# Hash attention and gated layers on one core: the first head prepared in halves, its hash weights on POOL, the second head scaled and rounded on ACT

## The chip, the core and the metric

The kernel runs on one core of a Trainium2 chip. Its engines run side by side: TensorE (PE, with its weight loads as PEld), VectorE (DVE), ScalarE (ACT), GpSimd (POOL) and SyncE (SP, which issues most transfers). Each takes its instructions in order and waits for the others through semaphores. The metric is the device time of one execution, in microseconds (us).

## What is computed

Attention over 4 batches of 8 heads (768 tokens, head size 64) with a mask from hash buckets, then two matrix products with a gate between them:

```python
q_bits = (np.einsum('bhsd,dk->bhsk', q, proj) > 0)      # 6 bits for each token; k alike
mask = q_bucket[:, :, :, None] == k_bucket[:, :, None, :]
scores = np.where(mask, scale * np.matmul(q, k.transpose(0, 1, 3, 2)), -1000000000.0)
attn = softmax(scores); x = np.matmul(attn, v)          # then (B*S, H*D) = (3072, 512)
h = x @ w_in; g = h * np.clip(h + 3.0, 0.0, 6.0) / 6.0  # 2048 wide
return g @ w_out
```

## The kernel before

PE multiplies in a rounded 32-bit format. Each factor is therefore held as a high part (the rounded value) and a low part (the rest), and a product is a sum of two or three matmuls. For head `i`, the tile `raw{i}` holds the transposed queries (rows 0 to 63) and keys (rows 64 to 127). `split_qk` makes from it four blocks of 128 x 768 in two tiles, `kk` (k1, k2) and `qq` (q1, q2): high parts, copies of them on the other rows, and low parts. `scale_q` multiplies the query rows by -1/8 first.

`hash_qk` multiplies these blocks with the projection: `pjl` (low parts) and `pjh` (high parts) are the stationary side, and the result `z` is made in two halves of 384 columns, three matmuls each (L330, L331, L332). `bits` turns the signs of `z` into rows 64 to 107 of q1 (L341, on DVE), and twelve of these rows are copied into k1 (L346, on ACT, for the first head; a transfer for the others). With these rows in place, one product of q1 with k1 (L376) gives score and mask together; q2 with k2 (L378) adds the low parts and does not need the bits.

The scores of one block of 128 queries, numbered `g`, go through a row of steps: `lowest` (L385, DVE, the minimum), `exponential` (L397, ACT), `transp` (L407, PE, six transposes), `split_p` (L464 on ACT, L468 on DVE, high and low part), `values` (L489, PE) and `output`. The loop over `k` works on several blocks at a time: in step `k` it transposes block `k`, starts the exponential of `k+1` and the scores of `k+3`. A head has six blocks. The hash of head `n` is issued when the scores of the fourth block of head `n-1` are, so head 1's stands on PE right behind the first six transposes. After the heads of one batch the two matrix products (`gemm1`, L634; `gemm2`, L673 to L678) are laid beside the next batch's heads.

The order on PE, DVE, ACT and POOL is the order of the code. The start is written out: 30 transposes of an identity matrix without use of the result (`NWARM`, L144), then `split_qk(0)`, `hash_qk(0)`, `bits(0)`, `scale_q(1)`, `split_v(0)` and three calls of `ahead`, the first of which calls `lead(0)` and with it `split_qk(1)`. For head 0, ACT and DVE make all blocks, and DVE makes the hash weights (`hash_weights`, L258 to L262) between two of its pieces. For head 1, POOL scales (L276, four pieces), rounds (L304) and makes the low parts (L318, four pieces for the keys, four for the queries); SP copies the rounded rows to the other half of the tiles.

## Time and profile before

| What | Value |
|---|---|
| Runs: median, lowest, highest | 1000.93, 998.02, 1001.17 us (3 runs) |
| The profiled execution: time, span | 998.6 us, 996.8 us |
| Busy share: PE, DVE, ACT, POOL | 96%, 74%, 63%, 50% |
| Chain that ended last: PE, DVE, issue, ACT, DMA, POOL | 61%, 17%, 6%, 5%, 4%, 4% |

PE is busy nearly all the time, and the chain of waits lies on it for most of the span. The busy time of PE is modelled and counts matmuls that overlap in its pipeline, so 96% does not mean that no more work would fit in. The shares are means over the whole span; what the change touches lies in the first 20 us, which have to be read by themselves.

### The profile page before, as it was taken

What the parts mean: (1) busy time and instruction counts of PE and PEld (TensorE: products, weight loads), DVE (VectorE), ACT (ScalarE), POOL (GpSimd) and SP (SyncE); (2) the same over time, 40 slices, a digit from 0 to 9 for tenths busy, and PEclk for the clock granted to TensorE, in tenths of its full rate; (3) what the DMA queues carried; (4) which work ended last, traced back from release to release, by engine and by line L of the source; (5) the groups of instructions that cost most, each with busy time, mean ns of one, the idle gap of its engine ahead of it and who ended that gap; (6) DMA issues with size and microseconds to landing.
All of it is one profiled execution on the core that took longest, in us unless ns stands there. A gap on an engine that the chain in (4) does not pass through costs nothing.

```text
span 996.8 us, 19354 instructions
## 1 busy us (share of the span) xinstructions
PE 960.7 (96%) x6330; PEld 876.2 (88%) x6330; DVE 739.9 (74%) x1439; ACT 632.2 (63%) x1419; POOL 495.6 (50%) x520
## 2 busy tenths in 40 slices
PE   8999999999999999799999999999999999999997
PEld 7999889888889998689989898898889989899996
DVE  7999988988579999777878878878877863243322
ACT  6889866555478887566666766666666663333332
POOL 6787735556546776455655654645645542100100
PEclk9999999999999999999999999999999999999999
DMA  4557679000044554488788787777788670101000
GB/s 120 145 151 178 155 213 379 9 2 1 7 131 115 122 122 122 129 231 240 225 260 246 219 252 224 227 234 226 236 236 239 197 215 14 43 1 43 1 22 22
DMA packets 109900, 148.38 MB, mean 149 GB/s; under 512 B 13364, under 2 KB 79284, under 8 KB 109800
## 3 DMA queue, kind: packets, MB, share of 16 engines
q1 hardware_dynamic: 105320, 141.64, 47.0%
q0 software_dynamic: 4480, 5.51, 4.4%
q8 instruction: 50, 0.82, 0.3%
q14 instruction: 50, 0.41, 0.1%
HBM read 75.76 MB, written 51.90 MB: 128 GB/s over the span
## 4 chain that ended last, share of the span: by engine, by line
PE 61%; DVE 17%; issue 6%; ACT 5%; DMA 4%; POOL 4%; SPq 3%; DVEq 0%; ACTq 0%; POOLq 0%
PE h L634 17%; PE acc L489 6%; PE pt L407 5%; PE po L678 5%; PE po L673 5%; PE po L674 5%; PE s L376 4%; PE s L378 4%; DVE p L385 4%; PE acc L501 4%; SPq L78 3%; DVE pl L468 3%; DMA px<-fd 2%; DVE gb L664 2%; POOL pl L466 2%
## 5 line engine op out<-in xcount | busy, mean ns | idle before, releaser
L397 ACT ACTIVATE p<-p,m 128x768 f32<-128x768 f32 x192 | 180.2, 939 | 90.7 <-DVE p L385 83.6
L385 DVE TENSOR_SCALAR_CACHE_REDUCE p<-s 128x768 f32<-128x768 f32 x192 | 182.9, 953 | 42.1 <-PE s L378 26.2
L656 DVE SCALAR_TENSOR_TENSOR g<-g,h 128x256 f32<-128x256 f32 x192 | 80.1, 417 | 104.8 <-ACT g L655 103.3
L655 ACT ACTIVATE g<-h,three 128x256 f32<-128x256 f32 x192 | 90.9, 473 | 94.9 <-PE h L634 80.2
L634 PE MATMUL h<-xh,w 128*128 128x256 f32 x1024 | 146.4, 283 | 2.9 <-ACT xh L624 2.9
L634 PEld LDWEIGHTS h<-xh,w 128*128 128x128 f32 x1024 | 135.7, 189 | 6.2 <-ACT xh L624 3.1
L466 POOL TENSOR_TENSOR pl<-spare,ph 128x384 fp32r<-128x384 f32 x43 | 58.9, 1370 | 120.2 <-ACT ph L464 84.1
L418 DVE STREAM_TRANSPOSE p<-p 128x768 f32<-128x768 f32 x86 | 84.0, 977 | 43.5 <-ACT p L397 43.5
L663 ACT CAST gb<-g 128x256 fp32r<-128x256 f32 x139 | 56.4, 406 | 80.4 <-DVE g L656 52.4
L468 DVE TENSOR_TENSOR pl<-pt,ph 128x384 fp32r<-128x384 f32 x204 | 104.0, 549 | 3.7 <-ACT ph L464 3.2
L376 PE MATMUL s<-kk,qq 76*128 76x384 f32 x384 | 101.5, 345 | 4.2 <-DVE qq L341 2.4
L464 ACT CAST ph<-pt 128x384 fp32r<-128x384 f32 x204 | 89.9, 474 | 17.5 <-PE pt L407 14.4
L378 PE MATMUL s<-kk,qq 128*128 128x384 f32 x384 | 100.1, 342 | 0.0
L673 PE MATMUL po<-w,gb 128*128 128x512 f32 x246 | 96.9, 394 | 0.4 <-ACT gb L663 0.4
L216 POOL TENSOR_TENSOR w<-wr,w 128x128 fp32r<-128x128 f32 x128 | 73.7, 609 | 47.2 <-ACT w L210 47.0
L674 PE MATMUL po<-w,gb 128*128 128x512 f32 x246 | 96.8, 394 | 0.0
L407 PE MATMUL pt<-ident,p 128*128 128x128 f32 x636 | 89.7, 274 | 5.9 <-DVE pl L468 4.4
L664 DVE TENSOR_TENSOR gb<-g,gb 128x256 fp32r<-128x256 f32 x136 | 77.8, 572 | 18.6 <-ACT gb L663 18.2
L407 PEld LDWEIGHTS pt<-ident,p 128*128 128x128 f32 x636 | 74.4, 140 | 15.0 <-PE pt L407 3.7
L634 PE MATMUL h<-xl,w 128*128 128x256 f32 x512 | 83.6, 283 | 2.6 <-POOL xl L625 2.2
L466 POOL TENSOR_TENSOR pl<-px,ph 128x384 fp32r<-128x384 f32 x43 | 56.1, 1304 | 56.7 <-ACT ph L464 42.7
L678 PE MATMUL po<-w,gb 128*128 128x512 f32 x246 | 78.2, 399 | 3.2 <-DVE gb L664 3.1
(156 smaller groups left out, 2167.8 us busy)
## 6 DMA issues: line engine op xcount, KB each, us to landing
fd<-p SPq DMA_DIRECT2D x86, 384.0 KB
spare<-fd SPq DMA_DIRECT2D x172, 96.0 KB
px<-fd SPq DMA_DIRECT2D x172, 96.0 KB
kk<-qq SPq DMA_DIRECT2D x62, 192.0 KB
wr<-in_w_in SPq DMA_DIRECT2D x16, 512.0 KB
wr<-in_w_out SPq DMA_DIRECT2D x16, 512.0 KB
raw<-in_qkT SPq DMA_DIRECT2D x20, 384.0 KB
vr<-in_v SPq DMA_DIRECT2D x32, 192.0 KB
```

What stands on the lines that cost most here:

```text
L376: nc.tensor.matmul(s[:, c, :HW], lhsT=q1[:KM, us], rhs=half(k1[:KM], c), start=True, stop=False)
L378: nc.tensor.matmul(s[:, c, :HW], lhsT=q2[:, us], rhs=half(k2, c), start=False, stop=True)
L385: nc.vector.tensor_scalar(out=pr_[:], in0=s[:, :, :HW], scalar1=CAP, scalar2=None, op0=ALU.min, op1=ALU.min, accum_out=m[:],)
L397: nc.scalar.activation(pr_[:], pr_[:], AF.Exp, bias=m[:], scale=-1.0, accum_out=sms[b][:, t, h : h + 1])
L407: nc.tensor.transpose(pt[:, x], probs[g][0][:, c, x * P : (x + 1) * P], ident[:])
L466: engine.tensor_sub(lo, pt, hi.bitcast(F32))
L468: lows.append(lambda: engine.tensor_sub(lo, pt, hi.bitcast(F32)))
L634: nc.tensor.matmul(hp[:], lhsT=wi[:, wp, wc], rhs=x[cc][xp], start=(k == 0 and cc == 0), stop=(k == 2 and cc == NCC - 1),)
L664: engine.tensor_sub(gl, g[:], gh.bitcast(F32))
L673: nc.tensor.matmul(po[u], lhsT=gh[:, us], rhs=wo[:, 0], start=(fc == 0), stop=False)
L674: nc.tensor.matmul(po[u], lhsT=gh[:, us], rhs=wo[:, 1], start=False, stop=False)
L678: nc.tensor.matmul(po[u], lhsT=gl[:, us], rhs=wo[:, 0], start=False, stop=(fc == NFC - 1))
```

## The change

The constant `NWARM` goes from 30 to 23. Of the steps for head 0: `hash_weights` runs on POOL, ahead of everything else of this head; ACT makes its three blocks in halves, in the order that the first half of the hash takes them; the bits of the first half are issued between the two halves of the hash; and the scores of head 0 take q2 with k2 first, then q1 with k1. Of head 1: ACT scales the queries in one piece and rounds both (L274, L305 of the new file), where POOL did. Lines move by up to four; the order of everything after the first two heads is the same as before.

```diff
-NWARM = 30
+NWARM = 23
...
     def hash_weights():
         for x in range(2):
             c = ZK + (1 - x) * NB
-            nc.vector.tensor_scalar_mul(pjh[:, c : c + NB], pr[:], (1.0, -1.0)[x])
+            nc.gpsimd.tensor_scalar_mul(pjh[:, c : c + NB], pr[:], (1.0, -1.0)[x])
         for r, c in ((slice(0, D), D), (slice(D, P), ZK)):
             pos = pjh[r, ZK + NB : ZM]
-            nc.vector.tensor_sub(pjl[r, c + NB : c + 2 * NB], pr[r], pos.bitcast(F32))
-            nc.vector.tensor_sub(pjl[r, c : c + NB], pos.bitcast(F32), pr[r])
+            nc.gpsimd.tensor_sub(pjl[r, c + NB : c + 2 * NB], pr[r], pos.bitcast(F32))
+            nc.gpsimd.tensor_sub(pjl[r, c : c + NB], pos.bitcast(F32), pr[r])
...
-        n = 4 if i <= 2 else 1
+        n = 4 if i == 2 else 1
...
-            if paced:
+            if paced or i == 1:
                 nc.scalar.mul(raws[i][:D, c], raws[i][:D, c], -SCALE)
...
         if i == 0:
 
+            hash_weights()
+            both = (slice(0, HW), slice(HW, S))
             nc.scalar.mul(q1[:D], raw[:D], -SCALE)
             nc.vector.tensor_copy(q1[D:], raw[D:])
-            for c in (slice(0, HW), slice(HW, S)):
+            for c in both:
                 nc.vector.tensor_sub(k2[:D, c], raw[D:, c], q1[D:, c].bitcast(F32))
-                if c.start == 0:
-                    hash_weights()
                 nc.vector.scalar_tensor_tensor(
                     out=q2[D:, c], in0=raw[:D, c], scalar=-SCALE, in1=q1[:D, c].bitcast(F32),
                     op0=ALU.mult, op1=ALU.subtract,
                 )
-            nc.scalar.copy(k2[D:], raw[D:])
-            nc.scalar.copy(q2[:D], q1[:D].bitcast(F32))
-            nc.scalar.copy(k1[:D], raw[D:])
+                nc.scalar.copy(k2[D:, c], raw[D:, c])
+                nc.scalar.copy(q2[:D, c], q1[:D, c].bitcast(F32))
+            for c in both:
+                nc.scalar.copy(k1[:D, c], raw[D:, c])
...
         for j in range(2):
+            if i == 0 and j:
+                bits(0, (0,))
...
-    def bits(i: int):
+    def bits(i: int, js=(slice(0, 2),)):
...
-        for c in range(2):
-            nc.tensor.matmul(s[:, c, :HW], lhsT=q1[:KM, us], rhs=half(k1[:KM], c), start=True, stop=False)
-        for c in range(2):
-            nc.tensor.matmul(s[:, c, :HW], lhsT=q2[:, us], rhs=half(k2, c), start=False, stop=True)
+        terms = [(q1[:KM], k1[:KM]), (q2, k2)]
+        if i == 0:
+            terms.reverse()
+        for n, (x, y) in enumerate(terms):
+            for c in range(2):
+                nc.tensor.matmul(s[:, c, :HW], lhsT=x[:, us], rhs=half(y, c), start=n == 0, stop=n == 1)
...
-            split_qk(n, nc.scalar.copy if ffn_on else nc.gpsimd.tensor_copy)
+            split_qk(n, nc.scalar.copy if ffn_on or n == 1 else nc.gpsimd.tensor_copy)
...
-        bits(0)
+        bits(0, (1,))
```

The order on ACT at the start, before (`qq_143` and `kk_142` are head 0's tiles, `p_197` is the first block of scores):

```order
L290 ACTIVATE qq_143<-raw_89 64x768 [waits DMAHW0_49]
L300 CAST kk_142<-raw_89 64x768
L301 CAST qq_143<-qq_143 64x768 [waits Activation_49]
L302 CAST kk_142<-raw_89 64x768
L346 CAST kk_142<-qq_143 12x384 [waits DVE_49] x2
L397 ACTIVATE p_197,sms_199<-p_197,m_196 128x768 [waits DVE_49]
```

And after (`raw_127` and `qq_171` are head 1's, the rest as above):

```order
L292 ACTIVATE qq_136<-raw_89 64x768 [waits DMAHW0_49]
L300 CAST kk_135<-raw_89 64x384
L301 CAST qq_136<-qq_136 64x384 [waits Activation_49]
L303 CAST kk_135<-raw_89 64x384 x2
L348 CAST kk_135<-qq_136 12x384 [waits DVE_49] x2
L274 ACTIVATE raw_127<-raw_127 64x768 [waits DMAHW3_49]
L305 CAST qq_171<-raw_127 128x768 [waits Activation_49]
L401 ACTIVATE p_190,sms_192<-p_190,m_189 128x768 [waits DVE_49]
```

The three whole copies have become six halves, and two instructions of head 1 now stand between the copy of the bits and the first exponential.

The order on POOL at the start, before (`raw_134`, `kk_177`, `qq_178` are head 1's, `vr_136` head 0's values):

```order
L276 TENSOR_SCALAR raw_134<-raw_134 64x192 [waits DMAHW3_49]
L356 CAST vv_174<-vr_136 128x6x64 [waits DMAHW4_49]
L357 TENSOR_TENSOR vv_174<-vr_136,vv_174 128x6x64 [waits Pool_49]
L304 CAST qq_178<-raw_134 128x768
L318 TENSOR_TENSOR kk_177<-raw_134,qq_178 64x192 [waits Pool_49]
L318 TENSOR_TENSOR qq_178<-raw_134,qq_178 64x192 x4
```

And after (`raw_127`, `kk_170` and `qq_171` are head 1's):

```order
L258 TENSOR_SCALAR pjh<-pr 128x6 [waits DMAHW2_49,DMAHW1_49,DVE_49]
L261 TENSOR_TENSOR pjl<-pr,pjh 64x6 [waits Pool_49]
L262 TENSOR_TENSOR pjl<-pjh,pr 64x6
L358 CAST vv_167<-vr_129 128x6x64 [waits DMAHW4_49,Pool_49]
L359 TENSOR_TENSOR vv_167<-vr_129,vv_167 128x6x64 [waits Pool_49]
L319 TENSOR_TENSOR kk_170<-raw_127,qq_171 64x192 [waits DMAHW3_49,Activation_49,Pool_49]
L319 TENSOR_TENSOR qq_171<-raw_127,qq_171 64x192 x4
```

POOL's scaling and rounding of head 1 are gone, the hash weights stand in front, and the first low part of head 1 waits for ACT.

The order on PE for head 0's hash and first scores, before:

```order
L330 MATMUL z_159<-qq_143,pjl 108x384 [waits DVE_49,Activation_49]
L331 MATMUL z_159<-kk_142,pjh 108x384 [waits Activation_49]
L332 MATMUL z_159<-qq_143,pjh 108x384 [waits DVE_49,Activation_49]
L330 MATMUL z_159<-qq_143,pjl 108x384
L331 MATMUL z_159<-kk_142,pjh 108x384 [waits DVE_49]
L332 MATMUL z_159<-qq_143,pjh 108x384 [waits DVE_49]
L376 MATMUL s_191<-kk_142,qq_143 128x384 [waits Activation_49] x2
L378 MATMUL s_191<-kk_142,qq_143 128x384 x2
```

And after (L382 stands for both products of the scores; the waits on ACT are those of q1 with k1):

```order
L333 MATMUL z_155<-qq_136,pjl 108x384 [waits DVE_49,Activation_49,Pool_49]
L334 MATMUL z_155<-kk_135,pjh 108x384 [waits DVE_49,Activation_49]
L335 MATMUL z_155<-qq_136,pjh 108x384 [waits DVE_49,Activation_49]
L333 MATMUL z_155<-qq_136,pjl 108x384 [waits DVE_49]
L334 MATMUL z_155<-kk_135,pjh 108x384 [waits Activation_49]
L335 MATMUL z_155<-qq_136,pjh 108x384 [waits Activation_49]
L382 MATMUL s_184<-kk_135,qq_136 128x384 [waits PE_49]
L382 MATMUL s_184<-kk_135,qq_136 128x384 [waits Activation_49] x2
```

The fourth matmul of the hash, which waited for nothing before, now waits for DVE, where the bits of the first half are the last instruction issued ahead of it.

## Rows read from the trace of the kernel before

**Rows 1.** Chain of waits, first 40 us: start us, us, what.

```profile
13.14 2.82 POOL qq L318 x4
...
16.00 0.43 PE z L332
```

**Rows 2.** Timeline of PE, 1 to 12 us: start us, us, engine, line, operation.

```profile
6.91 0.42 PE L330 MATMUL z<-qq,pjl 128*108 128x384 f32 x1
...
7.34 0.34 PE L332 MATMUL z<-qq,pjh 128*108 128x384 f32 x1
...
7.91 0.43 PE L332 MATMUL z<-qq,pjh 128*108 128x384 f32 x1
...
10.26 0.44 PE L376 MATMUL s<-kk,qq 76*128 76x384 f32 x1 [0.15 <-ACT kk L346]
10.54 0.51 PE L378 MATMUL s<-kk,qq 128*128 128x384 f32 x2
```

**Rows 3.** Timeline of ACT, 3 to 14 us.

```profile
3.85 0.84 ACT L290 ACTIVATE qq<-raw 64x768 fp32r<-64x768 f32 x1 [1.84 <-DMA raw<-in_qkT]
...
6.43 0.83 ACT L302 CAST kk<-raw 64x768 fp32r<-64x768 f32 x1
9.09 1.11 ACT L346 CAST kk<-qq 12x384 fp32r<-12x384 f32 x2 [1.82 <-DVE qq L341]
12.09 0.94 ACT L397 ACTIVATE p<-p,m 128x768 f32<-128x768 f32 x1 [1.89 <-DVE p L385]
```

**Rows 4.** Timeline of DVE, 3 to 14 us.

```profile
4.45 0.55 DVE L293 TENSOR_TENSOR kk<-raw,qq 64x384 fp32r<-64x384 f32 x1
...
5.57 0.16 DVE L262 TENSOR_TENSOR pjl<-pjh,pr 64x6 fp32r<-64x6 f32 x1
...
6.49 0.75 DVE L293 TENSOR_TENSOR kk<-raw,qq 64x384 fp32r<-64x384 f32 x1
7.27 0.58 DVE L296 SCALAR_TENSOR_TENSOR qq<-raw,qq 64x384 fp32r<-64x384 f32 x1
8.37 1.29 DVE L341 TENSOR_SCALAR qq<-z,thr,val 44x384 fp32r<-44x384 f32 x2 [0.52 <-PE z L332]
11.09 0.96 DVE L385 TENSOR_SCALAR_CACHE_REDUCE p<-s 128x768 f32<-128x768 f32 x1 [1.43 <-PE s L378]
...
13.42 0.97 DVE L196 SCALAR_TENSOR_TENSOR wr<-wr 128x512 uint32<-128x512 uint32 x1
```

**Rows 5.** Groups of instructions by shape: busy us, mean ns; POOL over the span.

```profile
L318 POOL TENSOR_TENSOR kk<-raw,qq 64x768 fp32r<-64x768 f32 x30 | 56.4, 1881 | 19.0 <-ACT qq L304 16.5
...
L318 POOL TENSOR_TENSOR qq<-raw,qq 64x192 fp32r<-64x192 f32 x4 | 2.8, 731 | 0.1
L318 POOL TENSOR_TENSOR kk<-raw,qq 64x192 fp32r<-64x192 f32 x4 | 2.3, 589 | 0.1
```

**Rows 6.** The same view for ACT.

```profile
L464 ACT CAST ph<-pt 128x384 fp32r<-128x384 f32 x204 | 89.9, 474 | 17.5 <-PE pt L407 14.4 <-PE acc L489 2.9
...
L304 ACT CAST qq<-raw 128x768 fp32r<-128x768 f32 x13 | 10.7, 824 | 0.0
L274 ACT ACTIVATE raw<-raw 64x768 f32<-64x768 f32 x12 | 10.1, 838 | 0.0
```

**Rows 7.** Unused transposes, two stretches (1.36:6, 6.2:7): ns min/median/max, first and last start.

```profile
L144 PE MATMUL warm<-ident x22: 381/421/477, 1.4 to 5.9; 128*128 128x128 f32 x22
...
L144 PE MATMUL warm<-ident x9: 272/273/381, 5.9 to 6.9; 128*128 128x128 f32 x9
```

**Rows 8.** Timeline of POOL, 3 to 19 us.

```profile
5.71 2.74 POOL L276 TENSOR_SCALAR raw<-raw 64x192 f32<-64x192 f32 x4 [4.39 <-DMA raw<-in_qkT]
...
10.83 2.26 POOL L318 TENSOR_TENSOR kk<-raw,qq 64x192 fp32r<-64x192 f32 x4
```

**Rows 9.** Timeline of PE, 405 to 425 us.

```profile
419.06 2.36 PE L634 MATMUL h<-xh,w 128*128 128x256 f32 x8 [2.90 <-ACT xh L624]
```

**Rows 10.** That stretch: us, busy PE PEld DVE ACT POOL, PEclk, DMA share, GB/s.

```profile
419.00:422.50 3.50, 3.44 (x14) 3.35 (x15) 2.32 (x3) 1.39 (x6) 1.60 (x2) 0.52 0.89 278
```

More of the change, by code (lines that the diff above doesn't have):

```diff
@@ L332, in hash_qk @@
             nc.tensor.matmul(z[:ZM, j, :HW], lhsT=pjq, rhs=q2[:, c], start=False, stop=True)
-    def bits(i: int):
+    def bits(i: int, js=(slice(0, 2),)):
         k1, k2, q1, q2 = state[i]
-        z = zs.pop(i)
-        for j in (range(2) if i == 0 else (slice(0, 2),)):
+        z = zs[i] if js == (0,) else zs.pop(i)
+        for j in js:
             c = slice(j * HW, (j + 1) * HW) if i == 0 else slice(0, S)
```

## The prediction

> **What bounds the kernel now.** I read the chain of waits first. Over the span it lies on PE for 61%, so a moment that PE loses at the start is not won back later unless PE waits for something that comes no later than before. The change touches only the first two heads, so I read that stretch alone. In the first 40 us the chain enters PE at 16.00 us: POOL's last low parts of head 1 (L318, 13.14 and 2.82 us long) release the last matmul of head 1's hash [rows 1]. That matmul stands on PE ahead of the scores of head 0's fourth block and of its second transposes, and from there the chain stays on PE with short stretches of DVE. **The start of head 0 is not on it**: DVE's first minimum waited 1.43 us for the scores and came at 11.09 us [rows 4], but what it led to stood behind the wait for POOL. The question is thus when POOL's eight low parts end after the change; the time of the whole kernel should move by about as much.
>
> **Before, the path to that point** is POOL's own queue: scaling from 5.71 us, values, rounding, then the low parts from 10.83 us [rows 8]. They take 5.13 us to 15.96 us [rows 1]. After, POOL has neither scaling nor rounding; the low parts wait for ACT's rounding of head 1 (L305), which stands on ACT behind the copies of head 0's bits. So I follow head 0's bits.
>
> **Hash weights on POOL.** They need two small transfers that are queued directly behind the first head's; the first head landed at 3.85 us [rows 3], and DVE could use the weights' transfers by 5.0 us, without a wait [rows 4]. Six instructions of 6 columns: on DVE 0.16 us each [rows 4]; on POOL no such row exists. From the two shapes of the low part, 1881 ns for 768 columns and 589 ns for 192 [rows 5], the slope is 2.24 ns a column and the fixed part 0.16 us, an estimate. So the bounds are 6 x 0.16 = 1.0 us and 6 x 0.589 = 3.5 us; I take 1.2 us with two waits among them, since the small shape is nearly all fixed part, and an end near 5.5 us (bounds 4.9 to 8.5 us). DVE loses these 0.7 us from its queue.
>
> The first scaling on POOL starts 0.09 us or less behind its wait and is no longer than the others (four in 2.74 us) [rows 8], so a first use costs nothing that shows. The Trainium skill (GPSIMD Engine Reference, 2.1 Instruction dispatch) says that the first call of a freshly loaded POOL function costs about 6 us that no instruction shows; the hash weights are now the first such calls. By that, an estimate from the page, the end would be near 11.5 us; by the row it is 5.5 us, and I go by the row.
>
> **First half of the hash.** The unused transposes start 0.214 us apart at first ((5.9 - 1.4)/21) and fall from 421 to 273 ns near 6.1 us [rows 7], which is the lower and then the higher of PE's two clock levels, 1.2 and 2.4 GHz. Number 23 starts at 1.4 + 22 x 0.214 = 6.1 us, so the shorter row of them ends just where the clock rose. Then three matmuls, 6.91 to 7.34 + 0.34 = 0.77 us [rows 2]: from 6.25 to 7.02 us, instead of 7.68 us. Their inputs are there: ACT's two halves at about 5.6 us (474 ns for one of 384 columns [rows 6] behind 3.85 + 0.84 us [rows 3]) and DVE's at 5.7 us.
>
> **Bits of the first half.** DVE has four low pieces from 4.45 us, 0.55 to 0.75 us each [rows 4], and is free near 7.05 us, no earlier than the hash. The bits are 1.29/2 = 0.65 us apart and 0.69 us long [rows 4]: 7.06 to 7.75 us.
>
> **Second half of the hash.** Its first matmul now waits for DVE, and by the order the last DVE instruction ahead of it is the bits of the first half. With 0.04 us for the signal: 7.79 us plus 0.80 us (0.77, and a longer first one after idling) = 8.59 us. Before, the last one ended at 7.91 + 0.43 = 8.34 us [rows 2]. So **this added wait makes the second half later by 0.25 us**, though the first is earlier by 0.66 us. The bits of the second half follow at 8.63 to 9.32 us (before: 8.37 + 1.29 = 9.66 us), their copy on ACT at 9.35 to 9.86 us (before: 9.09 + 1.11 = 10.20 us [rows 3]).
>
> **Scores of head 0.** The two matmuls without bits (0.51 us, [rows 2]) come under the wait for the bits; behind the copy there is one matmul, 0.44 us. DVE's first minimum starts at 9.91 + 0.44 + 0.04 = 10.39 us instead of 11.09 us, 0.7 us earlier. But ACT must first scale and round head 1, 838 and 824 ns [rows 6]: 9.88 to 10.72 us and 10.75 to 11.57 us. The first exponential follows at 11.60 us instead of 12.09 us [rows 3]. Queued behind the two are the exponentials; who waits for them are the first transposes, and they stand ahead of the stall on POOL.
>
> **Low parts of head 1.** They wait for 11.57 us, plus the signal: 11.61 us instead of 10.83 us. Their 5.13 us hold a clash: the four for the queries take 731 ns each, those for the keys 589 [rows 5], and a long DVE instruction of the weight conversion (L196, 0.97 us from 13.42 us) lies beside them [rows 4]. It still lies beside them after, so I keep 5.13 us: end at 16.74 us, and the last hash matmul of head 1 at 16.78 us instead of 16.00 us, **0.78 us later**. Without the clash it is 4 x 0.142 = 0.57 us less, 0.2 us later; the low bound. SP's copies of the rounded rows are issued when the rounding ends, thus 0.8 us later too; the matmul that needs the first of them ran before the one that waited for POOL, so they are not last. The transfers for the third head's inputs are queued ahead of them on SP and wait for head 0's pieces, which end no later. POOL's work for the third head moves by 0.8 us and has no one waiting.
>
> **The sum.** Off the path: seven transposes fewer, 0.7 us of DVE, the halves, the turned scores. On it: +0.78 us. The profiled execution took 998.6 us (span 996.8 us), so it would take 999.4 us. The median of the runs is 1000.93 us, 2.3 us above that execution; the forecast for a median is **1000.93 + 0.78 = 1001.7 us**. A measurement of this kernel can tell about 0.3%, 3 us, from no change, and the runs themselves spread over 3.15 us. So this is a case of no difference that shows.
>
> **Rivals.**
>
> *The fourth hash matmul does not wait for the bits*, only for DVE's low pieces (7.05 us). For it: the data that it reads are not those that the bits write. Against it: the order shows a new wait. Then the second half ends at 7.85 us, the bits follow each other and end at 8.4 us, ACT copies them by 8.97 us, and scaling and rounding end at 10.68 us; the low parts start at 10.72 us, 0.1 us earlier than before: 1000.8 us. With the clash gone as well it is 0.7 us earlier, 1000.2 us.
>
> *The hash weights are late on POOL* (the change does not do what it says). It decides from 6.2 us, where the unused transposes end. At the upper bound, 8.5 us, all that follows moves by 2.3 us: 1004.0 us. The clash above speaks for something of it, since DVE's low pieces run beside them; the columns speak against it. With the 6 us of the page named above the time would be near 1007 us; that case has its own chance below.
>
> *The clock falls, and the kernel is slower.* PE now has seven transposes fewer and a longer stall at head 1's hash (1.3 us more, as what stands before comes 0.5 us earlier and the end 0.8 us later). After an idle stretch of 2.90 us at 416 us [rows 9], PEclk was 0.52 over the next 3.5 us, though PE was busy for 3.44 of them [rows 10]: the lower level, and about half of 3.5 us, 1.7 us, lost. If the clock stayed low from 6.1 us, the two halves of the hash would take 0.45 us more each, and the dense work behind the stall 1.7 us more: 1001.7 + 0.9 + 1.7 = 1004.3 us, which is slower. It decides if the clock has not risen by 6.3 us or if the stall lets it fall. Against it: before, PE had nothing from 8.34 us until the first copy of the bits ended near 9.6 us [rows 2, 3], and the matmuls behind kept their short pitch, 0.51 us for two [rows 2]. The Trainium skill (TensorE: Matmul & The Clock Gate, Part 1) says that the low level is the state of rest and activity lifts it, at a moment that varies from run to run; that the clock rose only under the transposes agrees [rows 7], and by that rule some runs would pay a part of this price.
>
> **How the numbers follow.** The forecast (0.2 to 1.2 us later) gets 0.62, the fourth matmul without the wait 0.18, weights late by over a microsecond 0.07, the first call 0.02, the clock 0.08; 0.03 are left for the spread alone. The range goes from the lowest run with no shift, 998.0 us, to the highest with the forecast's upper shift and a part of the late weights, 1001.17 + 1.5 = 1002.7 us. Faster by over 0.3% (below 997.9 us) could only be the spread: 0.04. Slower (above 1003.9 us) takes the clock, the first call or the weights' upper bound: 0.08. The rest, 0.88, is no difference.
>
> **What would show it.** In the changed profile: 23 unused transposes whose duration falls near 6.1 us; the hash weights on POOL ending before 6.2 us; the first bits near 7.1 us and the second near 8.6 us (7.8 us would be the first rival); the first minimum near 10.4 us; ACT's rounding of head 1 ending near 11.6 us; the low parts ending near 16.7 us and the last matmul of head 1's hash right behind, with PE idle ahead of it. It is wrong if that matmul comes before 16.0 us, if PEclk is below 1 in the first 25 us, or if the two traces drift apart after 20 us by more than they differ there.

## The result and the profile after

| | Before | After |
|---|---|---|
| Median of 20 runs each, same chip | 999.87 us (997.75 to 1001.50) | 1001.62 us (998.84 to 1005.39) |
| After / before | | 1.0020, 95% interval 1.0012 to 1.0028 |
| Profiled execution: time, span | 998.6, 996.8 us | 1000.42, 998.6 us |
| Mean granted TensorE clock over the runs | 0.9954 to 0.9958 (103 later runs) | 0.9928 |

The changed kernel is slower by 0.2%, less than the 0.3% that the prediction called measurable, and the interval excludes no change. The start of its trace shows the whole path that the prediction followed. In the chain of waits (start us, us, what), POOL's low parts still release the last matmul of head 1's hash, as in [rows 1], but at 17.44 us:

```profile
15.73 1.66 POOL qq L319 x3
17.39 0.04 issue
17.44 0.65 PE z L335
18.09 1.28 PE s L382 x4
```

The timeline of POOL (start us, us, what; in brackets the idle time ahead and what ended it). The first five rows are the six hash weights, which stood on DVE in [rows 4]; the last two are the low parts of head 1, in the place of [rows 8]:

```profile
4.46 0.70 POOL L258 TENSOR_SCALAR pjh<-pr 128x6 fp32r<-128x6 f32 x2 [3.16 <-DVE qq L293]
5.12 0.58 POOL L261 TENSOR_TENSOR pjl<-pr,pjh 64x6 fp32r<-64x6 f32 x1
5.66 0.19 POOL L262 TENSOR_TENSOR pjl<-pjh,pr 64x6 fp32r<-64x6 f32 x1
5.92 0.41 POOL L261 TENSOR_TENSOR pjl<-pr,pjh 64x6 fp32r<-64x6 f32 x1
6.29 0.20 POOL L262 TENSOR_TENSOR pjl<-pjh,pr 64x6 fp32r<-64x6 f32 x1
...
12.11 2.98 POOL L319 TENSOR_TENSOR kk<-raw,qq 64x192 fp32r<-64x192 f32 x4 [3.56 <-issue]
15.14 2.24 POOL L319 TENSOR_TENSOR qq<-raw,qq 64x192 fp32r<-64x192 f32 x4
```

Of the timeline of PE, the two halves of head 0's hash (compare [rows 2]), then head 1's, whose matmuls wait for a transfer and twice for POOL, and the dense work behind it:

```profile
6.54 0.52 PE L333 MATMUL z<-qq,pjl 128*108 128x384 f32 x1
...
7.07 0.34 PE L335 MATMUL z<-qq,pjh 128*108 128x384 f32 x1
8.19 0.42 PE L333 MATMUL z<-qq,pjl 128*108 128x384 f32 x1 [0.78 <-DVE qq L343]
...
8.63 0.34 PE L335 MATMUL z<-qq,pjh 128*108 128x384 f32 x1
...
14.86 0.40 PE L334 MATMUL z<-kk,pjh 128*108 128x384 f32 x1 [0.85 <-DMA kk<-qq]
16.34 0.43 PE L335 MATMUL z<-qq,pjh 128*108 128x384 f32 x1 [1.08 <-POOL qq L319]
...
17.44 0.65 PE L335 MATMUL z<-qq,pjh 128*108 128x384 f32 x1 [0.33 <-POOL qq L319]
17.89 1.48 PE L382 MATMUL s<-kk,qq 128*128 128x384 f32 x4
19.17 1.48 PE L411 MATMUL pt<-ident,p 128*128 128x128 f32 x6
```

The timeline of ACT: the two copies of the bits, then scaling and rounding of head 1 and the first exponential (compare [rows 3]):

```profile
8.17 0.51 ACT L348 CAST kk<-qq 12x384 fp32r<-12x384 f32 x1 [0.36 <-DVE qq L343]
9.73 0.51 ACT L348 CAST kk<-qq 12x384 fp32r<-12x384 f32 x1 [1.05 <-DVE qq L343]
10.26 0.85 ACT L274 ACTIVATE raw<-raw 64x768 f32<-64x768 f32 x1
11.14 0.83 ACT L305 CAST qq<-raw 128x768 fp32r<-128x768 f32 x1
11.88 0.93 ACT L401 ACTIVATE p<-p,m 128x768 f32<-128x768 f32 x1
```

The timeline of DVE: the bits of the two halves and the first minimum (compare [rows 4]):

```profile
7.45 0.69 DVE L343 TENSOR_SCALAR qq<-z,thr,val 44x384 fp32r<-44x384 f32 x1 [0.55 <-PE z L335]
9.01 0.69 DVE L343 TENSOR_SCALAR qq<-z,thr,val 44x384 fp32r<-44x384 f32 x1 [0.88 <-PE z L335]
10.77 0.96 DVE L389 TENSOR_SCALAR_CACHE_REDUCE p<-s 128x768 f32<-128x768 f32 x1 [1.07 <-PE s L382]
```

One stretch, 17 to 24 us, in columns (us, then the busy time of PE, PEld, DVE, ACT and POOL with the number of instructions, PEclk, share of the transfer engines, GB/s), first of before and then of after:

```profile
17.00:24.00 7.00, 6.79 (x50) 6.15 (x49) 6.70 (x14) 5.96 (x13) 4.31 (x5) 1.00 0.13 29
```

```profile
17.00:24.00 7.00, 6.67 (x28) 6.37 (x28) 3.83 (x6) 3.04 (x7) 3.06 (x5) 0.51 0.03 5
```

PE is equally busy in both, but after has 28 matmuls in that time where before has 50: PEclk 0.51 is the lower of the two levels, 1.2 GHz, and it lies right on the dense work behind the stall.

**Where the time went in this pair of traces.** I match the minima on DVE, block by block (numbers from 0). After minus before: −0.32 us for the first block, +2.86 for block 3, +3.62 for block 7. Of the last, 1.44 us are the later last hash matmul (17.44 against 16.00), and the other 2.2 us come while the clock is low. The minimum of block 7 in the timelines of DVE, before, after and in `c_early2` (below):

```profile
26.25 0.96 DVE L385 TENSOR_SCALAR_CACHE_REDUCE p<-s 128x768 f32<-128x768 f32 x1 [0.24 <-PE pt L407]
```

```profile
29.87 0.96 DVE L389 TENSOR_SCALAR_CACHE_REDUCE p<-s 128x768 f32<-128x768 f32 x1 [0.24 <-PE pt L411]
```

```profile
26.36 0.96 DVE L387 TENSOR_SCALAR_CACHE_REDUCE p<-s 128x768 f32<-128x768 f32 x1 [0.24 <-PE pt L409]
```

From there the difference between after and before grows to 5.3 us at block 148 and 6.3 us at block 161, then it shrinks to 3.2 us at block 190 and to 1.8 us at the end of the span. This later part isn't the change's own: other kernels below, `b_hash` among them, show the same two swings against this trace of before (`b_hash`: +2.82 us at block 7, +5.58 at 148, +3.36 at 190, +2.0 for the span). What makes them stays open. Set against the trace of `c_early2`, which has the same later part, the changed kernel is 3.51 us late at block 7, 3.15 at block 128, 4.00 at block 190 and 4.3 at the end of the span: in this pair, what is lost in the start is not won back.

### The profile page after: what moved, and what is told of

Same layout as the page of the kernel before. It is cut to its first block, busy times and chain, and to the rows that moved or that the text cites. A ratio compares the mean times of both kernels' runs of the same rounds, so it can differ in the third digit from the quotient of the medians.

```text
span 998.6 us, 19341 instructions
## 1 busy us (share of the span) xinstructions
PE 963.3 (96%) x6323; PEld 880.0 (88%) x6323; DVE 739.3 (74%) x1433; ACT 635.0 (64%) x1424; POOL 495.1 (50%) x521
## 4 chain that ended last, share of the span: by engine, by line
PE 63%; DVE 16%; issue 5%; ACT 4%; DMA 4%; POOL 3%; SPq 3%; DVEq 0%; ACTq 0%; POOLq 0%
PE h L638 18%; PE s L382 9%; PE acc L493 6%; PE po L682 5%; PE pt L411 5%; PE po L677 5%; PE po L678 5%; PE acc L505 4%; DVE p L389 4%; SPq L78 3%; DVE pl L472 3%; DMA spare<-fd 2%; POOL pl L470 2%; DVE gb L668 2%; DVE wr L196 1%
## 5 line engine op out<-in xcount | busy, mean ns | idle before, releaser
L382 PE MATMUL s<-kk,qq 128*128 128x384 f32 (+1 forms) x768 | 172.2, 347 | 3.2 <-DVE qq L343 2.0
L382 PEld LDWEIGHTS s<-kk,qq 128*128 128x128 f32 (+1 forms) x768 | 135.0, 192 | 15.1 <-DVE qq L343 6.5
L668 DVE TENSOR_TENSOR gb<-g,gb 128x256 fp32r<-128x256 f32 x136 | 78.3, 576 | 18.3 <-ACT gb L667 17.8
```

The lines of the kernel that those rows point to most:

```text
L382: nc.tensor.matmul(s[:, c, :HW], lhsT=x[:, us], rhs=half(y, c), start=n == 0, stop=n == 1)
L668: engine.tensor_sub(gl, g[:], gh.bitcast(F32))
```

## Experiments

Three things are to be told apart: the gate (POOL's low parts of head 1 end later), the new wait between the halves of head 0's hash, and the clock. The kernels whose names begin with a are made from after, those with b from before, those with c go further. None leaves anything out. The table holds all of them, sorted by the last column; "gate" is the start of the last matmul of head 1's hash, "7 to 24 us" the granted clock there, both of the one profiled execution; "mean clock" is that of all timed runs, over the whole span.

| Kernel | Gate, us | Block 7, us | Clock, 7 to 24 us | Mean clock | Time / before, 95% |
|---|---|---|---|---|---|
| before | 16.00 | 26.25 | 1.00 | 0.9954 to 0.9958 | |
| `c_early2` | 16.16 | 26.36 | 0.90 | 0.9962 | 0.9980 (0.9970 to 0.9989) |
| `c_early` | 16.10 | 26.63 | 0.90 | 0.9958 | 0.9992 (0.9982 to 1.0003) |
| `c_dve` | 16.53 | 26.82 | 0.80 | 0.9945 | 0.9996 (0.9986 to 1.0006) |
| `b_hash` | 17.70 | 29.07 | 0.90 | 0.9947 | 1.0005 (0.9993 to 1.0018) |
| `b_act1` | 17.57 | 29.27 | 0.70 | 0.9942 | 1.0013 (0.9999 to 1.0028) |
| `a_order` | 17.79 | 28.02 | 0.90 | 0.9929 | 1.0014 (1.0003 to 1.0025) |
| `a_busy` | 18.81 | 29.02 | 0.80 | 0.9922 | 1.0014 (1.0000 to 1.0028) |
| `after2` | 18.41 | 28.62 | 0.80 | 0.9920 | 1.0015 (1.0003 to 1.0027) |
| after | 17.44 | 29.87 | 0.80 | 0.9928 | 1.0020 (1.0012 to 1.0028) |
| `a_warm30` | 18.28 | 30.35 | 0.70 | 0.9938 | 1.0020 (1.0011 to 1.0029) |
| `a_dve` | 17.55 | 29.01 | 0.70 | 0.9934 | 1.0021 (1.0007 to 1.0035) |
| `c_conv` | 17.02 | 27.90 | 0.90 | 0.9943 | 1.0028 (1.0015 to 1.0042) |
| `b_late` | 18.39 | 29.68 | 0.90 | 0.9929 | 1.0029 (1.0016 to 1.0041) |

The four kernels whose gate lies at 16.00 to 16.53 us have the four lowest times, and the ten with a gate of 17.02 us or later lie above them. Among these ten, the gate of the one profile doesn't order the times.

### The gate alone: `b_late`

The kernel before, with POOL's rounding of head 1 done three times:

```diff
-        copy(q1[:], raw)
+        for _ in range(3 if i == 1 else 1):
+            copy(q1[:], raw)
```

> The kernel before with POOL's rounding of head 1 done three times instead of once (same values), 1.65 us more ahead of the low parts and nothing else. T1: the last matmul of head 1's hash starts near 17.65 us instead of 16.00 us, the clock falls behind it as in the changed kernel, and the seventh block's minimum is at about 22.32 + 1.65 + 2.2 = 26.2 us; the time is 2 to 4 us above the kernel before. T2 (the number of transposes ahead): 30 stand here, so the clock stays at 1.00 and the minimum is at 24.0 us. A further rival, that a shift at the start is won back later: the time stays at that of the kernel before although the minimum is late.

Measured: slower by 0.29%, 2.9 us. POOL's rows, and the matmuls of PE that wait (both timelines):

```profile
10.47 2.60 POOL L305 CAST qq<-raw 128x768 fp32r<-128x768 f32 x3
13.16 2.88 POOL L319 TENSOR_TENSOR kk<-raw,qq 64x192 fp32r<-64x192 f32 x4
16.09 2.24 POOL L319 TENSOR_TENSOR qq<-raw,qq 64x192 fp32r<-64x192 f32 x4
```

```profile
17.29 0.65 PE L333 MATMUL z<-qq,pjh 128*108 128x384 f32 x1 [0.93 <-POOL qq L319]
...
18.39 0.66 PE L333 MATMUL z<-qq,pjh 128*108 128x384 f32 x1
```

The two more roundings are 1.73 us, and the queue began 0.5 us later here than in [rows 8]; the gate is 2.39 us later, block 7 is 3.43 us later, and the time follows. **So a later gate costs time**, with nothing else of the change in place, as the prediction read from [rows 1]. It didn't come without the clock: here too a stretch of low clock came, from 17.3 to 20.7 us, though the 30 unused transposes are all in place, and 1.04 of the 3.43 us come behind the gate.

### Moving head 1's scaling and rounding alone: `b_act1`

The kernel before, with these two steps of head 1 on ACT, whole:

```diff
-        n = 4 if i <= 2 else 1
+        n = 4 if i == 2 else 1
...
-            if paced:
+            if paced or i == 1:
...
-            split_qk(n, nc.scalar.copy if ffn_on else nc.gpsimd.tensor_copy)
+            split_qk(n, nc.scalar.copy if ffn_on or n == 1 else nc.gpsimd.tensor_copy)
```

> The kernel before with one part of the change alone: ACT scales and rounds head 1. By the prediction's steps the two stand behind the copy of the bits (10.20 us), end near 11.9 us, the low parts run from 12.0 us, and the last matmul of head 1's hash starts near 17.2 us, 1.2 us later than before; T1 adds a fall of the clock near 17 us and 2.2 us, so the seventh block's minimum is near 25.7 us, time 1 to 3 us above the kernel before. If ACT is not what delays the low parts, that matmul stays near 16.0 us.

Measured: 1.0013 (0.9999 to 1.0028), the low parts start at 12.34 us and the gate is at 17.57 us, 1.57 us later. The rows of ACT show why: what POOL did from 5.71 us on [rows 8] now stands behind the copies of the bits.

```profile
9.35 1.11 ACT L346 CAST kk<-qq 12x384 fp32r<-12x384 f32 x2 [1.94 <-DVE qq L341]
10.48 0.85 ACT L274 ACTIVATE raw<-raw 64x768 f32<-64x768 f32 x1
11.36 0.84 ACT L304 CAST qq<-raw 128x768 fp32r<-128x768 f32 x1
```

This one edit explains a later gate by itself; what the rest of the change is worth has to be read from how much of it the halves take back.

### The wait between the halves: `a_order`

The changed kernel, with the bits of both halves behind the whole hash:

```diff
-            if i == 0 and j:
-                bits(0, (0,))
...
         hash_qk(0)
+        bits(0, (0,))
         bits(0, (1,))
```

> The changed kernel with the bits of head 0's first half issued behind both halves of the hash, as before the change. The step of the prediction that the fourth hash matmul pays for waiting for the bits: the second half of the hash ends near 7.9 us instead of 8.97 us, the second bits start near 8.65 us instead of 9.01 us, the rounding on ACT ends near 11.6 us instead of 11.97 us and the last matmul of head 1's hash starts near 17.0 us instead of 17.44 us; about 0.4 us of the time, less than the spread shows. If the new wait costs nothing, that matmul stays at 17.4 us.

Measured: 1.0014. In this profile the hash weights ended later (7.36 us; see below), so I compare from their end to the end of the last bits: 2.69 us here, 3.22 us in after (6.48 to 9.70), 3.42 us in `after2` (7.43 to 10.85). **The new wait costs about 0.5 us rather than saving any**: taking the bits early puts 0.78 us of waiting into the second half (the row of 8.19 us in the timeline of PE after). The time is not distinguishable from after's. The rows of `a_order` on DVE (the bits), ACT (the rounding of head 1) and PE (the gate), from three timelines:

```profile
8.76 1.29 DVE L341 TENSOR_SCALAR qq<-z,thr,val 44x384 fp32r<-44x384 f32 x2 [2.02 <-PE z L333]
```

```profile
11.49 0.83 ACT L305 CAST qq<-raw 128x768 fp32r<-128x768 f32 x1
```

```profile
17.79 0.43 PE L333 MATMUL z<-qq,pjh 128*108 128x384 f32 x1 [0.34 <-POOL qq L319]
```

### The hash weights: `b_hash` and `a_dve`

`b_hash` is the kernel before with the weights on POOL (and ahead of its scaling), `a_dve` the changed kernel with them back on DVE:

```diff
-            nc.vector.tensor_scalar_mul(pjh[:, c : c + NB], pr[:], (1.0, -1.0)[x])
+            nc.gpsimd.tensor_scalar_mul(pjh[:, c : c + NB], pr[:], (1.0, -1.0)[x])
...
-            nc.vector.tensor_sub(pjl[r, c + NB : c + 2 * NB], pr[r], pos.bitcast(F32))
-            nc.vector.tensor_sub(pjl[r, c : c + NB], pos.bitcast(F32), pr[r])
+            nc.gpsimd.tensor_sub(pjl[r, c + NB : c + 2 * NB], pr[r], pos.bitcast(F32))
+            nc.gpsimd.tensor_sub(pjl[r, c : c + NB], pos.bitcast(F32), pr[r])
```

> The kernel before with the hash weights alone moved to POOL, ahead of its scaling. Nothing is left out. Theory (six columns on POOL take 0.2 to 0.6 us each beside DVE's two-input work, and wait for a small transfer that lands at 4.2 to 5.4 us): the six end at 6.3 to 7.6 us, POOL's scaling, rounding and low parts all start 0.5 to 1.5 us later, and the last matmul of head 1's hash comes at 16.5 to 17.5 us instead of 16.00. Time 0.5 to 1.5 us above the kernel before. Rival (the price on POOL is no more than the 1.2 us of the prediction): the six end by 5.7 us, the low parts end at 15.96 + at most 0.3 us, and the time is that of the kernel before.

Measured: the six take 2.2 us, and they start when the small transfer of the projection has landed, at 5.15 us here:

```profile
5.15 1.06 POOL L258 TENSOR_SCALAR pjh<-pr 128x6 fp32r<-128x6 f32 x2 [3.86 <-DMA pr<-in_proj]
6.17 0.57 POOL L261 TENSOR_TENSOR pjl<-pr,pjh 64x6 fp32r<-64x6 f32 x1
6.71 0.19 POOL L262 TENSOR_TENSOR pjl<-pjh,pr 64x6 fp32r<-64x6 f32 x1
```

They end at 7.32 us, the low parts start at 12.47 us (10.83 before) and the gate is at 17.70 us, 0.2 us beyond the end of what the theory gave. But the time is 1.0005 with an interval that reaches below 1: a gate that is 1.70 us later in the profile cost 0.3 us in the median. The interval, −0.7 to +1.8 us, holds the whole 1.70 us as well as nothing. One profile doesn't say when the transfer landed in the timed runs, so this stays a weak point of "the time moves by as much as the gate".

> The changed kernel with the hash weights alone put back on DVE, as the kernel before has them. Nothing is left out. Theory (DVE pays in its own queue what POOL no longer pays): the weights end near 5.8 to 6.2 us, but DVE's four low pieces, which the first bits stand behind, end 0.7 us later, near 7.45 us, where the first bits began in the changed kernel too; low parts of head 1 start within 0.2 us of 12.11 us and the last matmul of its hash comes within 0.3 us of 17.44 us; time within 0.7 us of the changed kernel's. Rival (the 2 us that the weights took on POOL instead of 1.2 are what made the gate 0.7 us later than predicted): first bits at 7.06 us, gate at 16.8 us, time 0.6 us or more lower.

Measured: 1.0021, as after. The weights end at 5.75 us, but DVE's low pieces now end at 7.70 us instead of 6.90, and the first bits begin right behind them, at 7.73 us (after: 7.45):

```profile
6.95 0.75 DVE L297 SCALAR_TENSOR_TENSOR qq<-raw,qq 64x384 fp32r<-64x384 f32 x1
7.73 0.69 DVE L344 TENSOR_SCALAR qq<-z,thr,val 44x384 fp32r<-44x384 f32 x1
```

The gate is at 17.55 us. **So in the changed kernel the place of the hash weights shows no gain**: on POOL the hash waits for them, on DVE the bits wait for the pieces behind them.

### The unused transposes: `a_warm30`

```diff
-NWARM = 23
+NWARM = 30
```

> The changed kernel with the 30 unused transposes of the kernel before instead of 23. Nothing is left out. Theory (the stall at head 1's hash lets the clock fall, not the missing transposes): the transposes end near 8 us, which lies ahead of what the hash waits for or delays it by at most 0.8 us; the last matmul of head 1's hash within 0.8 us of 17.44, a stretch at the lower clock still follows the stall in the profile or the mean granted clock stays near 0.993, and the time within 1 us of the changed kernel's. Rival (the seven transposes fewer are what lets the clock fall): no low clock before 400 us, mean granted clock back at 0.995 to 0.996, and the time 2 us or more below the changed kernel's.

Measured: 1.0020, as after; the mean clock over its runs is 0.9938, and its profile is at the lower level from 13.3 to 23.5 us. The seven transposes fewer are not what the changed kernel loses by.

### The clock: `a_busy` and `after2`

`a_busy` puts 18 unused transposes into the wait at head 1's hash, `after2` is the changed kernel once more with a second profile.

```diff
             nc.tensor.matmul(z[:ZM, j, :HW], lhsT=pjl[:], rhs=q1[:, c], start=True, stop=False)
+            if i == 1 and j == 0:
+                for _ in range(8):
+                    nc.tensor.transpose(z[:, 1, HW:], ident[:], ident[:])
             nc.tensor.matmul(z[:ZM, j, :HW], lhsT=pjk, rhs=k2[:, c], start=False, stop=False)
+            if i == 1 and j == 0:
+                for _ in range(10):
+                    nc.tensor.transpose(z[:, 1, HW:], ident[:], ident[:])
```

> The changed kernel with 18 more unused transposes in PE's wait at head 1's hash (8 behind its first matmul, 10 behind its second; their results stay unused). Theory T1 (the longer stall of PE ahead of head 1's low parts lets the clock fall at 17.0 us, and the dense work behind it then pays): the clock stays at 1.00 from 7 to 40 us, the last matmul of head 1's hash still starts near 17.4 us, the seventh block's minimum (25.65 us in the changed kernel, 22.32 us before) near 23.8 us, and the time is about 2 us below the changed kernel's, near 999.8 us. Rival T2 (the clock falls because only 23 transposes come ahead): the clock still falls near 17 us, the minimum stays near 25.6 us, time near 1001.6 us. Rival T3 (the low clock lies where PE has room): the clock stays up but the minimum stays within 0.5 us of 25.6 us.

Measured: 1.0014, mean clock 0.9922. It didn't test what it was made for: the clock was at the lower level from 8.7 to 15.6 us, ahead of the filling, and high behind it. The gate is at 18.81 us, since the weights ended at 7.6 us and the filling itself is on PE. No saving that shows.

> The changed kernel once more, unchanged: beside the next three on one chip, and with a second profile. Theory (the gate at POOL's low parts is set by the queues and so the same in every run, the moment of the low clock is not): head 1's last hash matmul again at 17.4 us, within 0.5 us (later by up to 1 us if the small transfer lands later); the stretch of low clock near the start again there but at another time than 17.02 to 23.85 us. Time 1.5 to 2.5 us above the kernel before's. Rival (the clock's fall is tied to the stall): it falls at 17.0 us again, within 0.3 us.

Measured: 1.0015. The low stretch is there, but from 9.3 to 16.1 us instead of 17.0 to 23.8 us. The weights start behind the transfer, and the hash waits for them:

```profile
5.31 1.01 POOL L258 TENSOR_SCALAR pjh<-pr 128x6 fp32r<-128x6 f32 x2 [4.02 <-DMA pr<-in_proj]
```

```profile
7.49 0.42 PE L333 MATMUL z<-qq,pjl 128*108 128x384 f32 x1 [1.21 <-POOL pjl L262]
```

So this gate is at 18.41 us, 1.0 us later than in the first profile, while block 7 is 1.25 us earlier (28.62 against 29.87): here the low clock lay ahead of the gate, where PE waits for POOL in the end, and not on the dense work behind it. **One profile of the start isn't the start**: a gate and a clock that both move by a microsecond or more from run to run have to be read from several. The Trainium skill (TensorE: Matmul & The Clock Gate, Part 1) says that the moment at which the clock rises varies from run to run. These two traces of one kernel agree: in the first all 23 unused transposes take 421 ns or more, in the second the shortest takes 273 ns. The fall, of which that sentence doesn't speak, differs by 7.7 us.

### Taking the gate away: `c_early`, `c_early2`, `c_dve`, `c_conv`

`c_early` keeps the changed kernel's steps and puts ACT's queue in another order: the four halves of head 0, then at once scaling and rounding of head 1, and only then head 0's key rows and the bits. The bits come behind both halves, as in `a_order`.

```diff
-            for c in both:
-                nc.scalar.copy(k1[:D, c], raw[D:, c])
+            k1_rows.append(lambda: [nc.scalar.copy(k1[:D, c], raw[D:, c]) for c in both])
...
-            if i == 0 and j:
-                bits(0, (0,))
...
-        if t == 0 and n < NJ:
+        if t == 0 and 1 < n < NJ:
...
         split_qk(0, None)
-        hash_qk(0)
-        bits(0, (1,))
         scale_q(1)
         split_v(0)
+        split_qk(1, nc.scalar.copy)
+        k1_rows.pop()()
+        hash_qk(0)
+        bits(0, (0,))
+        bits(0, (1,))
```

> The changed kernel with ACT's queue in another order: behind head 0's four halves ACT scales and rounds head 1 at once, and only then copies head 0's key rows and bits; the bits of both halves are also taken behind the whole hash of head 0, without the wait between the halves. Nothing is left out. Theory (the end of POOL's low parts sets the end of head 1's hash, and ACT's rounding sets the low parts): rounding ends near 7.5 us instead of 11.97, the low parts run from about 8.7 us (POOL has values to do first) to 13.9 us, and the hash of head 1 no longer waits for POOL; its last matmul comes near 14.9 to 15.5 us instead of 17.44, block 3's minimum 0.4 us ahead of the kernel before's, and since PE then stands shorter the low clock of 17 to 24 us is absent or later. Time 0.3 to 1 us below the kernel before, 1.5 to 2.5 below the changed one. Rival (the start is not what sets the time; the clock's moment alone is): the hash of head 1 comes earlier by 2 us and the time is still within 0.5 us of the changed kernel's. Second rival (the weight conversion on DVE bounds the start once POOL is out of the way): the gain at block 3 is below 0.3 us.

Measured: 0.9992 (0.9982 to 1.0003), and the same kernel again as `c_early2`:

> The kernel with head 1 scaled and rounded on ACT directly behind head 0's halves and the bits taken behind the whole hash, unchanged, once more. If the gate at POOL is what the changed kernel lost by, its time is again 2 to 3.5 us below the changed kernel's and 0 to 1.5 us below the kernel before's, with a mean granted clock of 0.995 to 0.996 against 0.993 of the changed kernel. If the first result was the spread, it comes within 1 us of the changed kernel's.

Measured: 0.9980 (0.9970 to 0.9989), 997.29 us against 999.49 us for before and 1000.17 us for `after2` beside it. Its rows on ACT, POOL and PE (three timelines of `c_early2`):

```profile
6.75 0.84 ACT L274 ACTIVATE raw<-raw 64x768 f32<-64x768 f32 x1
7.62 0.83 ACT L305 CAST qq<-raw 128x768 fp32r<-128x768 f32 x1
```

```profile
9.13 2.25 POOL L319 TENSOR_TENSOR kk<-raw,qq 64x192 fp32r<-64x192 f32 x4
11.44 2.46 POOL L319 TENSOR_TENSOR qq<-raw,qq 64x192 fp32r<-64x192 f32 x4
```

```profile
14.42 0.67 PE L331 MATMUL z<-qq,pjl 128*108 128x384 f32 x1
...
16.16 0.36 PE L333 MATMUL z<-qq,pjh 128*108 128x384 f32 x1
```

Rounding ends at 8.5 us instead of 11.97, the low parts at 13.9 us instead of 17.38, and the six matmuls of head 1's hash stand close together, with no wait for POOL. Against `a_order`, which differs in ACT's order alone, the mean clock goes from 0.9929 to 0.9958 and 0.9962, before's level, and the ratio from 1.0014 to 0.9992 and 0.9980. **That is the test of the cause**: with the wait for POOL at head 1's hash gone, the loss is gone, and the lower mean clock with it. The two profiles also part the gate from the clock: the low stretch is nearly the same in both (12.2 to 15.6 us in `a_order`, 12.3 to 15.7 us in `c_early`), and block 7 is still 1.39 us later in `a_order` (28.02 against 26.63), with a gate that is 1.69 us later. What I expected and did not see: block 3 is 0.1 to 0.4 us later than in the trace of before, not 0.4 us earlier. So the start of this one trace doesn't show why the median is up to 0.2% below before's. The trace of before has a clock of 0.998, at the top of its runs, whose mean is 0.9956; what its other runs lose, and where, no profile here shows. This stays open.

`c_dve` is `c_early` with the hash weights on DVE, by the same edit as `a_dve`.

> The same order of ACT and of the bits, with the six hash weights back on DVE, behind the first low piece. Nothing is left out. Theory (in this order the hash waits for the weights on POOL until 7.37 us, 1.4 us behind the last unused transpose): the weights end near 6.2 us, DVE's low pieces at 7.45 us, the hash of head 0 at 8.0 us instead of 8.73, the bits at 9.3 us instead of 10.06; ACT copies them to 10.3 to 10.5 us instead of 10.6, so the first minimum is only 0.1 to 0.3 us earlier, and the time within 0.5 us of the same order with the weights on POOL. Rival (the weights on POOL are what the start loses by): first minimum 0.7 us earlier and the time 0.7 us or more lower.

Measured: 0.9996. First minimum at 11.19 us (`c_early2`: 11.14) and bits 0.2 us earlier: no gain, since ACT's queue sets the copies of the bits. It is 1.6 us above `c_early2` beside it, but within 0.2 us of `c_early`'s median in the other set of runs, so I don't read a price of the place from it.

`c_conv` moves the first conversion of weights, two DVE steps of 1.4 us together, from the start into later steps:

```diff
-        for n, ks in enumerate(((1, 2, 6, 7, 8), (12, 14, 15, 18, 20, 21, 24), (24, 26, 27, 30, 32, 33, 36), (36, 38))):
+        for n, ks in enumerate(((3, 4, 5, 6, 7, 8, 9), (12, 14, 15, 18, 20, 21, 24), (24, 26, 27, 30, 32, 33, 36), (36, 38))):
...
-        for _ in range(2):
-            cv(0)
```

> As c_early, and the first weight conversion's two long DVE steps (L194, L196) are moved from the start to DVE's steps 3 to 9. Nothing is left out. Theory: DVE's minima of the first blocks no longer stand behind 1.7 us of conversion; block 3's minimum comes some 0.85 us ahead of the kernel before's, and the time is 0.5 to 1.5 us below it. Rival (what is gained at the start is taken by the later place of the conversion): the minima of blocks 3 to 5 are earlier by 0.8 us, and by block 10 no more than 0.3 us of it is left; time as c_early's.

Measured: 1.0028, slower than `c_early` beside it by 3.6 us. Block 3 is 1.23 us later than in before, not 0.85 earlier. The loss grows behind it, from 1.65 us at block 7 to 6.33 us at block 24, and the waits of PE between 24 and 75 us show where (line that waits, for what, us in total, times, longest):

```profile
PE acc L491 <- DVE pl L470: 3.1, 4, 2.1
```

`c_early` has 0.4 us on that row. Behind the longest of these waits the clock fell as well: PEclk is 0.62 from 51.5 to 56 us, 1.7 us of full clock, where `c_early` has no low stretch. In the start DVE has free time for these steps; in the loop PE waits for DVE's low parts behind them.

## Why the prediction was right, and where its steps were not

**The number and its two parts.** The forecast was 1001.7 us, the median 1001.62 us, and the change of 0.2% stays below the 0.3% that the prediction called measurable, as predicted. That the two medians agree is luck: the base, the median of three runs (1000.93), was 1.06 us above the median of 20 runs (999.87), and the shift was 1.75 us, not 0.78 (by the interval 1.2 to 2.8 us); the two errors cancel. Against the profiled execution, which the sum was made for, 999.4 us were predicted and 1000.42 us measured. The shift lies outside the forecast's own 0.2 to 1.2 us.

**The gate: right place, wrong size.** It was predicted at 16.78 us and came at 17.44 us in this trace, 0.66 us later. All of it can be followed in the rows above:

| Step | Predicted, us | After, us | Off by |
|---|---|---|---|
| Hash weights end on POOL | 5.5 | 6.48 | +1.0 |
| First hash matmul | 6.25 | 6.54 | +0.29 |
| Bits of the first half start | 7.06 | 7.45 | +0.39 |
| Second half starts | 7.79 | 8.19 | +0.40 |
| Rounding of head 1 ends on ACT | 11.57 | 11.97 | +0.40 |
| Low parts start | 11.61 | 12.11 | +0.50 |
| Low parts end | 16.74 | 17.38 | +0.64 |
| Last matmul of head 1's hash | 16.78 | 17.44 | +0.66 |

The term that was mis-sized is the hash weights: 2.0 us on POOL instead of 1.2. The bounds (1.0 to 3.5 us) held it; the choice near the lower end did not. Part of the 1.0 us was hidden behind the unused transposes, which ran to 6.51 us, where the prediction had the hash start at 6.25. The first half of the hash then took 0.87 us (6.54 to 7.41) instead of 0.77. So 0.4 us arrived at ACT, and from there every step kept its length. The low parts added 0.1 us at their start and 0.14 us in length: the long DVE instruction now lies beside the four for the keys (2.98 us) instead of those for the queries. And this profile was a mild one: in `after2` the weights began 0.85 us later, behind the transfer of the projection, in `a_warm30` 0.75 us later, and the gate was near 18.3 us. That the weights start behind this transfer was in the prediction; that their start varies by most of a microsecond was not. Had the term been right, nothing would follow for the choice of engine: `a_dve` loses as much on DVE.

**The new wait.** The order's wait was real, 0.78 us of PE's time, and the rival in which the fourth matmul doesn't wait is out. That rival's sum had a slip: with the second half done at 7.85 us, its bits start at 7.89 us and end at 8.58 us, not 8.4, and the low parts start level with before instead of 0.1 us earlier. The 0.25 us were the second half against the kernel before. Against the order without the wait, the prediction's figures give 0.74 us (second bits done at 9.32 against 8.58); `a_order` shows about 0.5 us.

**The clock.** This rival got 0.08. Its fall came true in the profile: PEclk 0.51 from 17 to 24 us, behind the stall, 2.2 us lost against 1.7 predicted for the dense work; its time, 1004.3 us, did not. The step that failed is the argument that before had held its level through a similar gap: it was one trace, taken at 0.998, where the mean over 103 runs of before is 0.9956. Every other profile of these experiments has a low stretch in the first 24 us, which begins at moments between 8.7 and 17.3 us.

The mean is lower with the change, 0.993 and 0.992 against 0.9956. It doesn't say where in the span: every profile has a second low stretch between 419 and 431 us, 3.4 us in the traces of before and `c_early2`, but 6.8 us in after and `after2`, as much as they have in the start. A drop of 0.003 to 0.004 over 998 us is 3 to 4 us if PE was the bound in all of it; the loss was 1.5 to 2 us. How much of that is gate and how much clock is separated only in part. `a_order` and `c_early` differ by 1.39 us at block 7 with nearly the same low stretch, so the gate costs by itself. `c_dve` has the gate away, a clock of 0.9945 and the time of before, and `b_late` has a gate 0.95 us behind after's in the two profiles and a clock no lower. So the clock belongs to the loss, and its share over all runs stays open.

**Late weights by a page's rule.** The first POOL instruction with `pr` starts at 4.46 us (its row names DVE's cast as what ended the wait), and the pair takes 0.70 us; in `after2` it starts at 5.31 us, right when the transfer lands. The Trainium skill (GPSIMD Engine Reference, 2.1 Instruction dispatch) gives about 6 us for the first call of a freshly loaded function; no row here shows such a time, and the low chance was right.

**Signs named beforehand.** Two of the three that were to make the prediction wrong came: PEclk below 1 in the first 25 us, and traces that drift apart after 20 us (+2.86 us at block 3, +3.62 at block 7). They were signs against the mechanism, and rightly so; the number held because the end of this trace and the base's error took the rest. The transposes, too, were to speed up near 6.1 us and did not in this profile.

**What hid as predicted.** Seven transposes fewer (`a_warm30`), the turned scores and the earlier first minimum (10.77 us against 11.09, predicted 10.39) bought nothing that shows: the stall behind POOL took it, as [rows 1] said. The turned scores were not run by themselves. The first exponential came at 11.88 us (predicted 11.60).

## What to carry to other kernels

Find the instruction that ends the start-up stall, and follow its own queue, before moving work off the engine that feeds it: an earlier first result is worth nothing when a later wait on the same engine stands. When a step is moved to another engine, its place in that queue counts for more than its engine: the same scaling and rounding on ACT gave a ratio of 1.0014 behind the bits (`a_order`) and 0.9992 and 0.9980 ahead of them (`c_early`, `c_early2`). Where a start depends on small transfers and on the clock's level, one profile is one draw; take two before a term of half a microsecond is read from it.

## What the hardware showed that was not expected

- The weights on POOL started at 4.46 us in one profile of the changed kernel and at 5.31 us in the other, behind the small transfer of the projection, though ACT began on the first head at 3.88 and 3.91 us.
- Instructions of six columns on POOL took from 0.19 to 0.60 us, against 0.16 us on DVE; the long ones lie beside DVE's two-input instructions of 0.55 to 0.60 us.
- In the first profile of the changed kernel all 23 unused transposes take 421 ns or more, where [rows 7] shows the last nine of before at 273 ns. That is the pace of the lower level: they start 0.214 us apart, and six transposes of the low stretch take 1.28 us in the chain of waits (at 19.37 us). Yet the profile's column of the granted clock says 1.00 from 1.5 to 7 us, in both kernels; in the start it can't be read without the instructions' own times. Their row over 1 to 7 us (ns min/median/max, first and last start):

```profile
L144 PE MATMUL warm<-ident x23: 421/421/474, 1.4 to 6.1; 128*128 128x128 f32 x23
```

- The clock's fall in the start came at 17.0 us in one profile of the changed kernel and at 9.3 us in the other. PE had worked on and off until then: its longest wait in the 5 us ahead of the fall was 1.08 us in the one and 1.21 us in the other.
